# A spectral and attention stack on one core: the memory check split among output tiles, short projection runs joined, and the spectrum's PSUM ring undone

## The chip, the cores and the metric

The kernel runs on one core of a Trainium2 chip. The metric is device time in microseconds (us) of one execution. Five engines work side by side, each through its own instructions in order: PE (TensorE: matmuls; its weight loads are listed as PEld), DVE (VectorE), ACT (ScalarE), POOL (GpSimd) and SP (SyncE, which issues transfers here). They wait for each other by semaphores. Matmul results go to PSUM, a small memory of banks; the kernel takes buffers in it from pools with tags, and a tag with `bufs=2` is a ring of two buffers: the third tile waits until the first has been read. S1 to S6 below are regions of SBUF that stages share.

## The reference

Four layers with a residual each: A, B, A, B. Layer A is a Fourier filter over tokens and features. Layer B is attention in 64 segments of 32 tokens, in which 8 memory rows pass from each segment to the next.

```python
def _A_ref(x, w_r, w_i):
    X = rfft2(x.astype(float32))
    X = X * (w_r + 1j * w_i)
    return irfft2(X, s=(S, D)).astype(bfloat16)

def _B_ref(x, mem0, Wq, Wk, Wv, Wo, seg_len):
    mem = mem0
    for s in range(n_seg):
        h = concatenate([mem, x[segment s]])
        q, k, v = h @ Wq, h @ Wk, h @ Wv            # 32 heads of 128
        p = softmax(where(mask, q @ k.T * scale, -1e9))
        o = (p @ v) @ Wo
        mem = o[:, :M]                              # the next segment's memory
        outs.append(o[:, M:])
    return concatenate(outs)

x = A_x                                             # (1, 2048, 640)
x = x + A(layernorm(x)); x = x + B(layernorm(x))
x = x + A(layernorm(x)); x = x + B(layernorm(x))
```

The kernel doesn't run layer B segment by segment. It guesses every segment's memory, computes all segments at once, and then checks that the memory rows it got agree with the guess to 1 in 100; a flag sends the program into a slower general path where they don't. This is the memory check.

## The kernel before

Layer A, spectrum. For each of eight indices j: matmuls along the features (`along_d`), sums and differences on DVE (`combine`), matmuls across (`across`), multiplication with the weights on DVE (`filt`), `products` on DVE and POOL, and matmuls back (`back`). The accumulators of the first two and X take their buffers from one ring of three.

```python
def along_d(j, o):
    ab[j, o] = ps = pp.tile([128, 2, 512], FP32, name=f"ab{o}", tag="pg", bufs=3)
    ...                                       # 10 matmuls of 321 columns; for o == 1 a copy to SBUF by ACT
def combine(j):                               # L320, L321 on DVE
    ...
def across(j, sg):
    X[j, sg] = x = pp.tile([128, 2, 512], FP32, name="X", tag="pg", bufs=3)
    ...                                       # 4 matmuls of 321 columns
def filt(j, sg):                              # L337: two multiplications of X with the weights on DVE
    ...
def products(j):
    ...
    nc.vector.tensor_tensor(out=a[:, 0, :, :], ..., op=ALU.subtract)                                # L343
    (nc.gpsimd if pos[j] < 6 else nc.vector).tensor_tensor(out=a[:, 1, :, :], ..., op=ALU.add)      # L344
    if j:
        nc.gpsimd.tensor_tensor(out=sd[j][:, 0:2, :], ...)                                          # L346
        nc.gpsimd.tensor_tensor(out=sd[j][:, 2:4, :], ...)                                          # L347

for i in range(8 + 3):                        # the order on PE, ACT and DVE is this one
    j, last, done = [self.SEQ[k] if 0 <= k < 8 else None for k in (i, i - 1, i - 3)]
    if j is not None: along_d(j, 1)
    if rest is not None: back(rest, (2,)) ...
    if last is not None: across(last, 0); filt(last, 0)
    if j is not None: along_d(j, 0); combine(j)
    if last is not None: across(last, 1); filt(last, 1); products(last) ...
    rest = done
    if done is not None: back(done, (0, 1))
```

Layer B, heads. Keys and queries of a head are projected in five runs of columns each, the last one short; dependent work of the two heads before (score parts, sums, value groups) is merged between them.

```python
kruns = [(0, 502), (512, 1007), (1024, 1519), (1536, 2035), (2048, 2176)]

def chain(w, hh, ps, src, lo, hi):            # five matmuls, L918
    ...
def k_run(w, h, g_):                          # chain into a PSUM tile (ring of 3), DVE copies it out (L977)
def q_run(w, h, g_):                          # chain into the same ring, ACT scales it out (L962 and smaller ones)
def score_part(h, P, part):                   # L994 into "pss" (ring of 2), ACT Exp (L997), DVE mask (L998)
def sums_wide(P, Rb, g_):                     # last head: L1043, then Ln and Exp on ACT (L1045, L1046)
def value_group(h, P, Rb, oT, g_):            # L1053 into "pso" (ring of 2), DVE scales it out (L1062 to L1066)

dense += [lambda g_=g_: k_run(w, h, g_) for g_ in range(NG)]         # NG = 5
...
    dense += [lambda g_=g_: q_run(w, h, g_) for g_ in range(NG)]
vt = [lambda t=t: v_tiles(w, h // 2, t) for t in range(0, NT, 2)]    # L984
dense += vt[5:] if h % 2 else vt[:5]
...
merge(dense, parts + [g1[0], post[0], g1[1], post[1], g1[2], post[2], g1[3], g1[4]])   # spread evenly
...
elif h == H:                                  # after the last head: output tiles begun as filling
    merge(begin(), parts)
    b1 = begin()
    wide[0](); wide[1]()
    merge(b1[0:3], wide[2:5]); merge(b1[3:], groups)
    post[0]()
else:
    merge(begin(), groups)
```

Layer B, end. The check runs first, then the 16 output tiles (two half tiles of 32 matmuls each, L1209, added to x on DVE, L1219). In the first layer B each tile is normed and its first matmuls for the next layer A follow (`stage1_tile`, L273).

```python
def _b_mem_check(...):
    for c in range(5):
        for h in range(H):                    # 32 matmuls of 71 columns, L692
            nc.tensor.matmul(ps[:, :NM], lhsT=Wo_sb[:, h, c * 128:(c + 1) * 128], rhs=oTm[:, h, 0:NM], ...)
        for lo, hi, guess in gq_of(c):        # the guess subtracted on DVE, L697
            nc.vector.tensor_tensor(out=dl[:, lo:hi], in0=ps[:, lo:hi], in1=guess, op=ALU.subtract)
        nc.scalar.activation(out=sq[:], in_=dl[:], func=ACTF.Square)               # L700
        nc.scalar.activation(out=n2[:], in_=ps[:, 0:NC], func=ACTF.Square)         # L701
        nc.tensor.matmul(pe2[:, 0:NC], lhsT=ones_c[:, 0:1], rhs=sq[:], ...)        # L702
        nc.tensor.matmul(pn2[:, 0:NC], lhsT=ones_c[:, 0:1], rhs=n2[:], ...)        # L703
    ...                                       # verdict on DVE; range of the sums, L716 to L720

for t in range(16):                           # _FastOut.run
    for k in (2 * t, 2 * t + 1):
        self.accumulate(ps, k, lhs, ...)      # L1209
        nc.vector.tensor_tensor(out=x[:, t, c0:c0 + 320], in0=ps[:, 0:320], in1=x[...], op=ALU.add)
    if nxt is None: nc.sync.dma_start(out=self.xd[:, t, :], in_=x[:, t, :]); continue
    if t: nxt.stage1_tile(pa, "pss", xns[(t - 1) % 3], t - 1)
    ...                                       # statistics and norm of tile t
if nxt is not None: nxt.stage1_tile(pa, "pss", xns[15 % 3], 15)
```

Of the kernel before, what the change touches and what calls it, by code (L numbers as in the profile page):

```python
# [148 lines left out]
class _Cut:  # L149

    def __init__(self, t):
        self.t, self.o = t, 0
# [39 lines left out]
class LayerA:  # L192
# [83 lines left out]
    def spectrum(self, late_loads=()):  # L276
# [19 lines left out]
        self.pp = pp = tc.alloc_tile_pool(name=f"{self.lname}_ps2", bufs=1, space=PSUM)  # L296
# [4 lines left out]
        def along_d(j, o):  # L301
            ab[j, o] = ps = pp.tile([128, 2, 512], FP32, name=f"ab{o}", tag="pg", bufs=3)
            for ch in range(5):
                for c in range(2):
                    nc.tensor.matmul(ps[:, 1 - c if o else c, 0:NF], lhsT=YT[:, ch, 2 * j + c, :, :].rearrange("p s k -> p (s k)"), rhs=Fd[:, ch, o, :],  # L305
                                     start=(ch == 0), stop=(ch == 4))
            if o == 1 and j:
                ab[j, o] = dbs
                nc.scalar.copy(out=dbs, in_=ps[:, :, 0:NF])
# [13 lines left out]
        def across(j, sg):  # L323
            X[j, sg] = x = pp.tile([128, 2, 512], FP32, name="X", tag="pg", bufs=3)
# [14 lines left out]
        def products(j):  # L339
# [3 lines left out]
            nc.vector.tensor_tensor(out=a[:, 0, :, :], in0=t1[:, :, 0, :], in1=t2[:, :, 0, :], op=ALU.subtract)  # L343
            (nc.gpsimd if pos[j] < 6 else nc.vector).tensor_tensor(out=a[:, 1, :, :], in0=t1[:, :, 1, :], in1=t2[:, :, 1, :], op=ALU.add)  # L344
# [4 lines left out]
        def back(j, chunks):  # L349
            for ch in chunks:  # L350
                f0, f1 = CH[ch]
                m = f1 - f0
                if j == 0 and ch == 1:
                    psu = pp.tile([128, 2, 512], FP32, name="psu0", tag="pg", bufs=3)[:, 0, :].rearrange("p (e c k) -> p e c k", e=2, c=2)
                else:
                    psu = pp.tile([128, 2, 2, 128], FP32, name="psu2", tag="pu", bufs=2)
# [9 lines left out]
                for e in range(2):  # L366
                    (nc.vector.tensor_copy if j == 0 and ch == 1 else nc.scalar.copy)(out=UT[0:m, ch, e, :, j * 16:j * 16 + 16].rearrange("p s (c k) -> p s c k", c=2),
                                                                                in_=psu[0:m, e, :, :].rearrange("p c (s k) -> p s c k", k=8))

        with tc.manual_schedule(engines={nc.tensor.engine, nc.scalar.engine, nc.vector.engine}):  # L370
            rest = None
            for i in range(8 + 3):
                j, last, done = [self.SEQ[k] if 0 <= k < 8 else None for k in (i, i - 1, i - 3)]
                if j is not None:
                    along_d(j, 1)
                if rest is not None:
                    back(rest, (2,))
                    for _ in range(2):
                        if late:
                            late.pop(0)(UT[0:1, 0, 0, 0, rest * 16:rest * 16 + 1])  # L380
# [6 lines left out]
                if last is not None:  # L387
                    across(last, 1)
                    filt(last, 1)
# [3 lines left out]
                rest = done  # L393
                if done is not None:
                    back(done, (0, 1))
            back(rest, (2,))
            for f in late:
                f(UT[0:1, 0, 0, 0, 112:113])

    def tokens(self, x_dst, xn_dst, handoff=None):  # L400
# [8 lines left out]
        pp = self.pp  # L409
# [266 lines left out]
def _b_mem_check(tc, g, pj, pc, wk, oTm, mnb, gq_of, NM, NC, flag_col, sums=None):  # L676
    nc = tc.nc
    Wo_sb, ones_c = g["Wo_sb"], g["ones_c"]
    pe2, pn2 = pc[0][0:1, :], pc[1][0:1, :]
    cut = {}  # L680

    def tmp(name, p, n, dt=FP32):
        if not isinstance(wk, _Cut):
            return wk.tile([p, n], dt, name=name, tag=name, bufs=1)[:]
        if name not in cut:
            cut[name] = wk.f32(n) if dt == FP32 else wk.bf(n)
        return cut[name][0:p, :]

    for c in range(5):
        ps = pj.tile([128, 512], FP32, name="psm", tag="pj")  # L690
        for h in range(H):
            nc.tensor.matmul(ps[:, :NM], lhsT=Wo_sb[:, h, c * 128:(c + 1) * 128], rhs=oTm[:, h, 0:NM], start=(h == 0), stop=(h == H - 1))  # L692
        if mnb is not None:
            nc.scalar.copy(out=mnb[:, c, :], in_=ps[:, :NM])
        dl = tmp("dl", 128, NC)
        for lo, hi, guess in gq_of(c):
            nc.vector.tensor_tensor(out=dl[:, lo:hi], in0=ps[:, lo:hi], in1=guess, op=ALU.subtract)  # L697
        sq = tmp("sq", 128, NC, BF16)
        n2 = tmp("n2", 128, NC, BF16)
        nc.scalar.activation(out=sq[:], in_=dl[:], func=ACTF.Square)  # L700
        nc.scalar.activation(out=n2[:], in_=ps[:, 0:NC], func=ACTF.Square)  # L701
        nc.tensor.matmul(pe2[:, 0:NC], lhsT=ones_c[:, 0:1], rhs=sq[:], start=(c == 0), stop=(c == 4))  # L702
        nc.tensor.matmul(pn2[:, 0:NC], lhsT=ones_c[:, 0:1], rhs=n2[:], start=(c == 0), stop=(c == 4))  # L703
    e2 = tmp("e2", 1, NC)
    nc.vector.tensor_copy(out=e2[:], in_=pe2[:, 0:NC])
    viol = tmp("viol", 1, NC)
    nc.vector.scalar_tensor_tensor(out=viol[:], in0=pn2[:, 0:NC], scalar=-(CONV_TOL ** 2), in1=e2[:], op0=ALU.mult, op1=ALU.add)
    vmax = tmp("vmax", 1, 1)
    nc.vector.tensor_reduce(out=vmax[:], in_=viol[:], axis=AX.X, op=ALU.max)
    if sums is None:  # L710
        nc.vector.tensor_single_scalar(out=flag_col, in_=vmax[:], scalar=0.0, op=ALU.is_gt)
        return
    accR, accS = sums
    okw = tmp("okw", 128, accR.shape[1])
    ok2 = tmp("ok2", 128, 2, BF16)
    nc.vector.tensor_single_scalar(out=okw[:], in_=accR, scalar=INV_MAX, op=ALU.is_le)  # L716
    nc.vector.tensor_reduce(out=ok2[:, 0:1], in_=okw[:], axis=AX.X, op=ALU.min)
    nc.vector.tensor_single_scalar(out=okw[:], in_=accS, scalar=SUM_MAX, op=ALU.is_le)
    nc.vector.tensor_reduce(out=ok2[:, 1:2], in_=okw[:], axis=AX.X, op=ALU.min)
    nc.tensor.matmul(pe2[:, 0:2], lhsT=ones_c[:, 0:1], rhs=ok2[:], start=True, stop=True)  # L720
    ok = tmp("okq", 1, 2)
    nc.vector.tensor_single_scalar(out=ok[:], in_=pe2[:, 0:2], scalar=127.5, op=ALU.is_ge)
    okm = tmp("okm", 1, 1)
    nc.vector.tensor_reduce(out=okm[:], in_=ok[:], axis=AX.X, op=ALU.min)
    nc.vector.tensor_single_scalar(out=vmax[:], in_=vmax[:], scalar=0.0, op=ALU.is_le)
    nc.vector.tensor_tensor(out=vmax[:], in0=vmax[:], in1=okm[:], op=ALU.mult)
    nc.vector.tensor_single_scalar(out=flag_col, in_=vmax[:], scalar=0.5, op=ALU.is_lt)
# [38 lines left out]
def _b_full_pass(tc, g, lay, env, flag_col):  # L766
# [86 lines left out]
    with octx:  # L853
# [3 lines left out]
        _b_mem_check(tc, g, pj, (pcs[:, 0, :], pcs[:, 1, :]), wk, oTm, mnb, lambda c: [(0, lay.NC, gq[:, c, MR:NSEG * MR])], lay.NM, lay.NC, flag_col)  # L857
# [10 lines left out]
def _b_fast_pass(tc, g, bs, env, flag_col, nxt=None):  # L868
# [32 lines left out]
    if True:  # L901
# [198 lines left out]
        with tc.manual_schedule(engines={nc.tensor.engine, nc.scalar.engine, nc.vector.engine}):  # L1100
            for h in range(H + 2):
# [11 lines left out]
                if h < H:  # L1113
                    dense += [lambda g_=g_: k_run(w, h, g_) for g_ in range(NG)]
                    if h < 2:
                        dense.append(lambda: q_m(w, h))
                    else:
                        dense += [lambda g_=g_: q_run(w, h, g_) for g_ in range(NG)]
# [391 lines left out]
```

## Time and profile before

| | |
|---|---|
| time, median of 3 | 1636.85 us (1634.64 to 1639.93) |
| span of the profiled execution | 1635.0 us |
| PE busy | 1555.4 us, 95% |
| ACT, DVE, POOL busy | 51%, 49%, 17% |
| first spectrum, then tokens | about 35 to 92, 92 to 135 us |
| first layer B: heads, output tiles | about 135 to 687, 687 to 833 us |
| second spectrum, tokens | about 834 to 891, 891 to 938 us |
| second layer B: heads, output tiles | about 938 to 1490, 1490 to 1635 us |

A line of the timeline gives start, length, engine, line of the kernel, operation, what is written and read, its size and the count, and in brackets how long the engine stood idle before it and what ended that. Lengths of single matmuls overlap, so starts are compared. In the list of waits each line says who waited for whom, total us, times and the longest. "Issue" is idle time for which the profile shows no releaser.

### The profile page before, as it was taken

What the parts mean: (1) busy time and instruction counts of PE and PEld (TensorE: products, weight loads), DVE (VectorE), ACT (ScalarE), POOL (GpSimd) and SP (SyncE); (2) the same over time, 40 slices, a digit from 0 to 9 for tenths busy, and PEclk for the clock granted to TensorE, in tenths of its full rate; (3) what the DMA queues carried; (4) which work ended last, traced back from release to release, by engine and by line L of the source; (5) the groups of instructions that cost most, each with busy time, mean ns of one, the idle gap of its engine ahead of it and who ended that gap; (6) DMA issues with size and microseconds to landing.
All of it is one profiled execution on the core that took longest, in us unless ns stands there. A gap on an engine that the chain in (4) does not pass through costs nothing. (4 is left out here: it accounts for less than half of the span.)

```text
span 1635.0 us, 36218 instructions
## 1 busy us (share of the span) xinstructions
PE 1555.4 (95%) x14240; PEld 1072.1 (66%) x14241; DVE 800.1 (49%) x2254; ACT 836.4 (51%) x2522; POOL 275.7 (17%) x262
## 2 busy tenths in 40 slices
PE   4898999999999999899987899999999999999998
PEld 2566666666666667677755666666666667666775
DVE  5973454555545554533358625555545554544110
ACT  5374666666666666511124746666666666663000
POOL 0520121212121212100024101212121212111000
PEclk9999999999999999999999999999999999999999
DMA  4472334334434343824202713434434343446241
GB/s 157 145 278 87 100 134 144 135 135 139 151 117 154 117 161 121 268 93 118 77 15 95 257 31 126 135 135 140 151 117 153 118 160 122 140 144 214 69 132 52
DMA packets 167873, 218.05 MB, mean 133 GB/s; under 512 B 7374, under 2 KB 141836, under 8 KB 159756
## 3 DMA queue, kind: packets, MB, share of 16 engines
q1 hardware_dynamic: 167084, 213.34, 39.1%
q8 instruction: 113, 1.85, 0.5%
q0 software_dynamic: 608, 2.30, 0.4%
q14 instruction: 68, 0.56, 0.1%
HBM read 170.52 MB, written 45.09 MB: 132 GB/s over the span
## 5 line engine op out<-in xcount | busy, mean ns | idle before, releaser
L918 PEld LDWEIGHTS <-bB_S 128*128 128x128 bf16 x3180 | 261.1, 97 | 184.4 <-issue 4.3
L1062 DVE TENSOR_TENSOR bB_S<-pso,bB_S 128x480 bf16<-128x480 f32 (+1 forms) x320 | 189.4, 592 | 265.9 <-PE pso L1053 251.6
L997 ACT ACTIVATE bB_S<-pss 128x269 bf16<-128x269 f32 (+5 forms) x576 | 213.6, 385 | 192.6 <-PE pss L994 180.4
L1209 PE MATMUL psx<-Wo_sb,bB_S 128*128 128x320 bf16 x2048 | 288.2, 299 | 3.0 <-DMA bB_S<-oTx_d 3.0
L977 DVE CAST bB_S<-psk 128x495 bf16<-128x495 f32 (+3 forms) x320 | 191.4, 599 | 123.0 <-PE psk L918 92.3
L1209 PEld LDWEIGHTS <-bB_S 128*128 128x128 bf16 x2048 | 197.2, 98 | 79.6 <-DMA bB_S<-oTx_d 3.7
L998 DVE TENSOR_TENSOR bB_S<-bB_S,maskf 128x269 bf16<-128x269 bf16 (+5 forms) x576 | 163.0, 287 | 153.1 <-ACT bB_S L997 149.3
L1022 POOL TENSOR_TENSOR bB_S<-bB_S,bB_S 128x634 f32<-128x634 f32 x64 | 98.0, 1531 | 786.5 <-ACT bB_S L1018 786.5
L986 ACT CAST bB_S<-psv 128x512 bf16<-128x512 f32 (+1 forms) x288 | 160.5, 557 | 84.4 <-PE psv L984 84.1
L962 ACT ACTIVATE bB_S<-psq 128x480 bf16<-128x480 f32 x300 | 152.5, 508 | 98.8 <-PE psq L918 98.8
L918 PE MATMUL psk<-B2hT_S,bB_S 128*128 128x495 bf16 (+3 forms) x800 | 165.4, 343 | 2.3 <-DVE bB_S L977 2.1
L918 PE MATMUL psk<-B1hT_S,bB_S 128*128 128x495 bf16 (+3 forms) x800 | 165.3, 343 | 0.6 <-DVE bB_S L977 0.4
L984 PE MATMUL psv<-bB_S,B1hT_S 128*128 128x256 bf16 x1360 | 163.4, 273 | 0.2 <-DVE bB_S L977 0.2
L984 PE MATMUL psv<-bB_S,B2hT_S 128*128 128x256 bf16 x1360 | 163.4, 273 | 0.2 <-DVE bB_S L977 0.2
L994 PEld LDWEIGHTS <-bB_S 128*128 128x128 bf16 x1216 | 102.8, 97 | 90.5 <-issue 6.2
L918 PE MATMUL psq<-B2hT_S,bB_S 128*128 128x495 bf16 (+5 forms) x780 | 158.1, 336 | 0.1
L918 PE MATMUL psq<-B1hT_S,bB_S 128*128 128x495 bf16 (+5 forms) x780 | 158.0, 336 | 0.1
L994 PE MATMUL pss<-bB_S 128*128 128x132 bf16 (+8 forms) x1216 | 147.8, 215 | 2.8
L984 PEld LDWEIGHTS <-B2hT_S 128*128 128x128 bf16 x1360 | 128.8, 98 | 13.6 <-issue 0.3
L984 PEld LDWEIGHTS <-B1hT_S 128*128 128x128 bf16 x1360 | 128.8, 98 | 13.5 <-issue 0.3
L1053 PE MATMUL pso<-bB_S,bB_S 128*128 128x132 bf16 (+8 forms) x1216 | 119.6, 216 | 0.0
L1053 PEld LDWEIGHTS <-bB_S 128*128 128x128 bf16 x1216 | 91.2, 98 | 15.9 <-DVE oTmf L1063 0.5
(245 smaller groups left out, 1544.7 us busy)
## 6 DMA issues: line engine op xcount, KB each, us to landing
bB_S<-Rd SPq DMA_DIRECT2D x62, 1059.5 KB
oTx_d<-bB_S SPq DMA_DIRECT2D x60, 512.0 KB
bB_S<-oTx_d SPq DMA_DIRECT2D x56, 512.0 KB
bB_S<-in_B_Wq_dram SPq DMA_DIRECT2D x32, 320.0 KB
bB_S<-in_B_Wk_dram SPq DMA_DIRECT2D x32, 320.0 KB
bB_S<-in_B_Wv_dram SPq DMA_DIRECT2D x32, 320.0 KB
bB_S<-oTx_d SPq DMA_DIRECT2D x14, 384.0 KB
Wo_sb<-in_B_Wo_dram SPq DMA_DIRECT2D x4, 1280.0 KB
```

The costliest lines, as they stand in the source:

```text
L918: nc.tensor.matmul(ps, lhsT=w[:, ch, hh * 128:(hh + 1) * 128], rhs=src[:, ch, lo:hi], start=(ch == 0), stop=(ch == 4))
L962: nc.scalar.mul(out=qv[:, :, 0:SEG], in_=x_view(ps, o, n)[:, :, 1:SW], mul=scale)
L977: nc.vector.tensor_copy(out=KTs[h % 2][:, lo:hi], in_=ps[:, 0:hi - lo])
L984: nc.tensor.matmul(ps[:, i * 256:(i + 1) * 256], lhsT=hT[:, ch, st.hcol((t + i) * 128):st.hcol((t + i) * 128) + 128], rhs=w["Wv"][:, ch, : ...
L986: nc.scalar.copy(out=V[:, t:t + n, :].rearrange("p a b -> p (a b)"), in_=ps[:, 0:n * 256])
L994: nc.tensor.matmul(ps[:, off - o0:off - o0 + hi - lo], lhsT=KT[:, t * 128:(t + 1) * 128], rhs=QT[:, lo:hi], start=True, stop=True)
L997: nc.scalar.activation(out=E[:, 0:n], in_=ps[:, 0:n], func=ACTF.Exp)
L998: nc.vector.tensor_tensor(out=P[:, o0:o0 + n], in0=E[:, 0:n], in1=bs.mask[:, o0:o0 + n], op=ALU.mult)
L1022: nc.gpsimd.tensor_tensor(out=accS, in0=accS, in1=sums_sb, op=ALU.add)
L1053: nc.tensor.matmul(pso[:, lo - q0:hi - q0], lhsT=V[:, t, (h % 2) * 128:(h % 2 + 1) * 128], rhs=P[:, off:off + hi - lo], start=(i == 0), st ...
L1062: nc.vector.tensor_tensor(out=oT.rearrange("p (r s j) -> p r s j", r=16, j=2)[:, :, s0:s0 + ns, :], in0=byclass(po), in1=rx, op=ALU.mult)
L1209: self.tc.nc.tensor.matmul(ps[:, 0:320], lhsT=lhs(h, k // 2), rhs=self.g["Wo_sb"][:, h, c0:c0 + 320], start=(h == 0), stop=(h == H - 1))
```

## The change

Three things differ. (1) In layer B's heads the short key run is put into one item with the first long one, and so is the short query run; the order after the last head has more filling between the wide sums. (2) The memory check becomes a class with pieces: `prepare` and `begin` among the first output tiles, `block` and `vote` for each of the five parts. The guess is subtracted by a matmul with minus the identity into the same accumulator, the square is taken from PSUM, and the tolerance is applied to the guess, whose squares are made early. In the last layer all five parts stand among output tiles; in the first, two do, and three come after the last tile, ahead of its `stage1_tile`. The output loop now has a fixed order. (3) The spectrum of layer A has separate accumulators (ab0, ab1 and X, one buffer each) in place of the ring of three, does `back` in one go, and gives L343 to POOL for the first six indices; tokens use a pool of their own.

```diff
-            ab[j, o] = ps = pp.tile([128, 2, 512], FP32, name=f"ab{o}", tag="pg", bufs=3)
+            ab[j, o] = ps = pp.tile([128, 2, 512], FP32, name=f"ab{o}", tag=f"ab{o}")
...
-            X[j, sg] = x = pp.tile([128, 2, 512], FP32, name="X", tag="pg", bufs=3)
+            X[j, sg] = x = pp.tile([128, 2, 512], FP32, name="X", tag="X")
...
-            nc.vector.tensor_tensor(out=a[:, 0, :, :], in0=t1[:, :, 0, :], in1=t2[:, :, 0, :], op=ALU.subtract)
-            (nc.gpsimd if pos[j] < 6 else nc.vector).tensor_tensor(out=a[:, 1, :, :], in0=t1[:, :, 1, :], in1=t2[:, :, 1, :], op=ALU.add)
+            (nc.gpsimd if pos[j] < 6 else nc.vector).tensor_tensor(out=a[:, 0, :, :], in0=t1[:, :, 0, :], in1=t2[:, :, 0, :], op=ALU.subtract)
+            (nc.gpsimd if j else nc.vector).tensor_tensor(out=a[:, 1, :, :], in0=t1[:, :, 1, :], in1=t2[:, :, 1, :], op=ALU.add)
...
-                if rest is not None:
-                    back(rest, (2,))
...
                 if last is not None:
                     across(last, 1)
+                if i >= 3:
+                    done = self.SEQ[i - 3]
+                    back(done)
...
+                if last is not None:
                     filt(last, 1)
                     products(last)
...
+    def begin(self, acc=None):
+        if acc is not None:
+            nc.tensor.matmul(self.pe[:, self.NC:self.NC + 2], lhsT=self.g["ones_c"][:, 0:1], rhs=self.ok2[:], start=True, stop=True)
+        for c in range(5):
+            nc.tensor.matmul(self.pe[:, 0:self.NC], lhsT=self.g["minus_c"][:, 0:1], rhs=self.n2[:, c, :], start=(c == 0), stop=False)
+
+    def block(self, c):
...
         for h in range(H):
+            nc.tensor.matmul(ps[:, :NM], lhsT=self.g["Wo_sb"][:, h, c * 128:(c + 1) * 128], rhs=self.oTm[:, h, 0:NM], ...)
...
+        for i, (lo, hi, guess) in enumerate(guesses[:n]):
+            nc.tensor.matmul(ps[:, lo:hi], lhsT=self.minus[:], rhs=guess, start=False, stop=(i == n - 1), ...)
+        nc.scalar.activation(out=sq[:], in_=dl[:, 0:NC], func=ACTF.Square)
+
+    def vote(self, c):
+        self.tc.nc.tensor.matmul(self.pe[:, 0:self.NC], lhsT=self.g["ones_c"][:, 0:1], rhs=self.squares[c][:], start=False, stop=(c == 4))
...
-                    dense += [lambda g_=g_: k_run(w, h, g_) for g_ in range(NG)]
+                    def both(run):
+                        return [lambda: (run(w, h, NG - 1), run(w, h, 0))] + [lambda g_=g_: run(w, h, g_) for g_ in range(1, NG - 1)]
+                    dense += both(k_run)
+                    dense += [lambda: q_m(w, h)] if h < 2 else both(q_run)
...
-                    b1 = begin()
-                    wide[0]()
-                    wide[1]()
-                    merge(b1[0:3], wide[2:5])
-                    merge(b1[3:], groups)
+                    fill = begin()
+                    for i, f in enumerate(wide):
+                        f()
+                        for _ in range(2):
+                            (fill or groups).pop(0)()
...
+        early = {t: c for c, t in enumerate((3, 5) if nxt is not None else (3, 5, 7, 9, 11))}
...
+            if t == 2:
+                check.prepare(acc)
+            if t == 4:
+                check.begin(acc)
+            if t in early:
+                check.block(early[t])
+            if t - 1 in early:
+                check.vote(early[t - 1])
...
         if nxt is not None:
+            for c in range(len(early), 5):
+                check.block(c)
             nxt.stage1_tile(pa, "pss", xns[15 % 3], 15)
+            for c in range(len(early), 5):
+                check.vote(c)
+            check.result(flag_col, True)
```

## The prediction

> **What bounds the kernel now.** I read the page first, then busy time by stage, then the timeline inside the stages that the change edits, then the list of waits.
>
> ```profile
> PE 1555.4 (95%) x14240; PEld 1072.1 (66%) x14241; DVE 800.1 (49%) x2254; ACT 836.4 (51%) x2522; POOL 275.7 (17%) x262
> ```
>
> TensorE is busy 95% of the span and no other engine passes 51%. Where the missing 5% lie is told by the stages (columns: stretch, its length, then busy time of PE, PEld, DVE, ACT, POOL, the granted clock, DMA share, GB/s):
>
> ```profile
> 145.00:640.00 495.00, 492.71 (x4552) 331.98 (x4549) 244.95 (x731) 308.31 (x977) 88.71 (x58) 1.00 0.38 130
> ...
> 834.00:891.00 57.00, 47.29 (x316) 32.17 (x316) 48.28 (x57) 18.56 (x54) 29.16 (x24) 0.92 0.14 43
> ...
> 938.00:1460.00 522.00, 517.63 (x4793) 348.06 (x4793) 253.63 (x756) 321.56 (x1018) 91.77 (x60) 1.00 0.37 128
> ```
>
> The attention heads (the two long stretches, two thirds of the time) are TensorE alone: a matmul of 502 columns starts every 0.21 us. The spectrum (834 to 891) is a hand-over between PE and DVE: each is busy about 48 of 57 us. So in the heads only PE stalls and PE work count, and in the spectrum it is the length of the cycle PE, DVE, POOL.
>
> In the heads the timeline of PE shows one stall, in every second head:
>
> ```profile
> 1031.31 0.45 PE L918 MATMUL psk<-B2hT_S,bB_S 128*128 128x128 bf16 x5
> 1031.59 0.65 PE L994 MATMUL pss<-bB_S 128*128 128x141 bf16 x4
> 1032.08 1.22 PE L918 MATMUL psq<-B2hT_S,bB_S 128*128 128x502 bf16 x5
> ```
>
> The four score matmuls take 0.49 us to the next start; four such without a stall, at 670.92, take 0.23. They are two score parts in a row, only 0.28 us (the short key run) after the part before them; scores have two PSUM buffers, and the second part needs the one that ACT's Exp is still reading. The list of waits counts these:
>
> ```profile
> PEld L994 <- issue: 6.2, 30, 0.2
> ```
>
> Thirty, that is 15 heads in each layer. At the end of layer B the memory check stands alone on PE (layer 1 shown):
>
> ```profile
> 687.36 1.17 PE L692 MATMUL psm<-oTmf,Wo_sb 128*128 128x71 bf16 x31
> 689.60 0.19 PE L692 MATMUL psm<-oTmf,Wo_sb 128*128 128x71 bf16 x1 [1.07 <-DVE oTmf L1066]
> ...
> 694.65 1.21 PE L692 MATMUL psm<-oTmf,Wo_sb 128*128 128x71 bf16 x32
> ...
> 700.46 0.16 PE L720 MATMUL pc<-bB_S,ones_c 128*1 128x2 bf16 x1
> 700.56 3.30 PE L1209 MATMUL psx<-Wo_sb,bB_S 128*128 128x320 bf16 x23
> ...
> 829.31 0.44 PE L273 MATMUL ps<-bB_S 128*128 128x128 bf16 x5
> 832.64 0.72 PE L273 MATMUL ps<-bB_S 128*128 128x128 bf16 x5 [2.89 <-DVE bB_S L127]
> ```
>
> From 687.36 to 700.46 PE holds the check and 20 output matmuls, with waits on DVE and ACT in every block; 32 check matmuls alone take 1.2 us. At the other end PE idles 2.9 us for the norm of the last tile, and the next layer's first 20 matmuls then run at 0.28 us each instead of 0.14 (they span 833.98 to 839.5). The spectrum's cycle:
>
> ```profile
> 856.95 2.20 DVE L343 TENSOR_TENSOR A2gt_S<-A2tmp_S 128x642 f32<-128x642 f32 x1
> 859.08 1.54 DVE L337 TENSOR_TENSOR A2tmp_S<-X,A2tab_S 128x642 f32<-128x642 f32 x2
> ...
> 856.93 1.54 POOL L344 TENSOR_TENSOR A2gt_S<-A2tmp_S 128x642 f32<-128x642 f32 x1 [0.37 <-DVE A2tmp_S L337]
> ```
>
> DVE's L343 takes 0.83 when it runs first and 2.20 when POOL's L344 (1.54) started just before it; then the next product of X, and through the ring PE, come late. The step was 5.26 us (848.57 to 853.83) and becomes 6.71 (860.55 to 867.26).
>
> [...] 0.28 for 0.14 us after 2.9 us of idleness, and no fall inside the check, where PE has gaps of about 1 us at most. [...]
>
> **The change, part by part.**
>
> *Heads.* Key run 4 goes ahead of run 0 as one item, and so does query run 4. The list has 12 or 13 items for 17 dependent ones in place of 14 or 15, so more pairs of dependents stand together, but each pair now follows at least a long run (1.05 us) after the previous part, and Exp takes 0.4. The 30 stalls go: 30 x (0.49 - 0.23) = 7.8 us. No matmul is added or removed.
>
> *Check, layer 1.* I walk PE on the clock of the old trace. Up to 673.1 nothing differs. Each wide sum is now followed by two output items (1.09 us) in place of one, so PE doesn't wait for Ln and Exp (1.2 us a sum): about 1.1 us. The wait of PE for head 30's reciprocals (DVE at 679.39) stays. L716 and L717 (1.3 us) no longer stand between the last evictions, so those end at about 688.1, not 689.4. Then 41 output matmuls (1+4+4+32) at 0.136 end the fourth half tile at 693.8; in the old trace it ends at 703.7. Gain 9.9. Given back: two blocks of 32 matmuls at 33 ns plus two subtractions, 1.12 each, and seven votes at 0.12: 3.1. Three blocks (3.4) go where PE idled from 829.6 to 832.6, and the last stage-1 matmuls, votes and DVE's read of the vote bank delay the spectrum by about 0.6. But PE no longer idles, so I expect the full clock: 20 matmuls x 0.14 = 2.7 gained. Sum: 9.9 - 3.1 - 0.6 + 2.7 = 8.9 us.
>
> *Check, layer 2.* The same 9.9, less five blocks (5.6), votes and openings (1.2), all in the body: 3.1 us.
>
> *Spectrum, twice.* X gets one buffer of its own: PE can fill it only when DVE has left it, so DVE idles 0.85 us a step (0.06 + 4 x 0.138 + 0.2), as long as the L343 that goes to POOL. [...] POOL has 1.5 + 1.5 + 1.3 + 1.3 = 5.6 us a step, PE has 1.38 + 0.37 (wait) + 0.55 + 1.77 (the three chunks of "back" in one go, with 0.3 for a buffer) + 1.38 + 0.55 = 6.0. So 6.0 in place of 6.7 on four steps: 2.9 us. At the end "back" of index 7 waits for POOL, about as now. The walk gives 2.9 us a spectrum; as it hangs on POOL times that I have not seen together, I count 2.0: 4.0 us for both.
>
> Sum: 7.8 + 8.9 + 3.1 + 4.0 = 23.8; 1636.85 - 23.8 = 1613.
>
> **Rivals.**
>
> *The spectrum gets longer.* If POOL's L343 and L344 take 2.2 rather than 1.54 (the longest in the trace), POOL needs 7.0 a step and lags; "back" and the products of the last indices wait. For it: POOL has four operations a step and the chain crosses three engines with one X. Against it: POOL's 1.54 is steady where DVE isn't in its way. It would cost about 3 us each where I count 2 gained: 1623.
>
> *The stall in the heads moves.* The short query run's three small ACT evictions now come ahead of the long run's, just before two score parts in a row; if Exp is late there, the same 0.26 returns. For it: ACT has about 2 us of work in that stretch. Against it: by the durations in the old trace the buffer is free 0.1 to 0.2 us in time. It would make 1621.
>
> *A hidden transfer shows.* The output stage starts 10 us earlier, but its tables are issued only after the last head's values (DFT table at 688.6), and the DMA engines are full until 705. The first stage-1 matmuls would come at 693.8. For it: that issue time doesn't move. Against it: that table is the first in the queue. It could take 0 to 5 us from layer 1: up to 1618.
>
> **Range and chances.** All three rivals together come to about 1636, unlikely at once; one of the first two is 1621 to 1623. If instead the spectrum gives the full 2.9 (1.8 more in all) and the clock stays up in further places (it also stands below full, at 0.84, from 880.7 to 891.5 and at 0.85 from 82.6 to 94.0), 1605 to 1608. Eight in ten: 1603 to 1625. Faster by 2% means below 1604.1: 0.12. Slower by 2%, above 1669.6, needs a new wait of 55 us: 0.02. Within 2%: 0.86.
>
> **What would show it.** Heads: "PEld <- issue" on the score line falls from 30 to about 0. Check: no stretch of PE with check matmuls alone; three blocks just before the last stage-1 matmuls; first 20 spectrum matmuls at 0.14. Spectrum: combine to combine 6.0 us, L343 on POOL at 1.54. The prediction is wrong if score matmuls still wait, if stage 1 of tile 0 waits for a DMA, or if POOL operations take 2 us.

## The result and the profile after

The changed kernel takes 1619.08 us (median of 4 runs, 1614.60 to 1620.72) beside 1636.61 us for the kernel before; the ratio is 0.9887 with a 95% interval of 0.9859 to 0.9914. That is 17.5 us gained where the prediction summed 23.8. The profiled execution of the changed kernel is the longest of its four, span 1619.0 us against 1635.0. Its busy times, from the page:

```profile
PE 1548.0 (96%) x14260; PEld 1068.8 (66%) x14261; DVE 777.2 (48%) x2219; ACT 836.0 (52%) x2530; POOL 295.7 (18%) x278
```

Matmuls are up by 20 and PE's busy time is down by 7.4 us (1555.4 before), the span by 16.1. So some 8.7 us of idle time went, and the rest is time that was counted as busy: a score matmul that stands for its buffer counts as busy while it stands (0.65 in place of 0.40 us for four, 30 times). The stretches between fixed points of PE's program, read from the starts of single matmuls in both traces, say where the time came from:

| stretch (us) | before | after | gain | predicted |
|---|---|---|---|---|
| heads of layer 1, first key matmul to first output matmul | 515.30 | 511.12 | 4.2 | 3.9 |
| heads of layer 2 | 517.25 | 512.79 | 4.5 | 3.9 |
| first to 129th output matmul, layer 1 | 35.72 | 29.90 | 5.8 | 9.9 |
| the same, layer 2 | 34.90 | 29.00 | 5.9 | 9.9 |
| 129th to last output matmul, layer 1 | 125.20 | 128.04 | -2.8 | -3.1 |
| the same, layer 2 | 121.57 | 128.38 | -6.8 | -6.8 |
| last output matmul of layer 1 to 21st transform of layer A | 10.13 | 7.66 | 2.5 | 2.1 |
| first spectrum, first transform to first inverse matmul | 57.10 | 57.93 | -0.8 | 2.0 |
| second spectrum, 21st transform to first inverse matmul | 52.18 | 51.71 | 0.5 | 2.0 |
| first inverse matmul to first key matmul, both layers | 122.91 | 119.56 | 3.4 | 0 |

Heads, check pieces and the end of layer 1 came as predicted. Two things did not: the start of the output stage gained 6 us a layer in place of 10, and the spectra gained nothing. A line that the prediction did not have, 3.4 us after the spectra, hides part of that; 2.8 of it lie in layer 2, where 20 query matmuls ran partly at half clock before (5.98 us, granted clock 0.72 from 938.1 to 944.1) and don't now (1.00 from 926.9 to 931.3), a difference of 1.6.

The score line in the groups of PE's weight loads (columns: count, busy us, mean ns, idle before, and what ended it) has no "issue" item left, where the waits before counted 6.2 us in 30 times:

```profile
L1013 PEld LDWEIGHTS <-bB_S 128*128 128x128 bf16 x1216 | 99.7, 97 | 84.4
```

PE's timeline (start, length, what, count, and in brackets the idle time before and its releaser), at the end of the heads, at the first product of layer A's first stage (L273), and at the end of layer 1:

```profile
677.51 0.45 PE L1233 MATMUL psx<-Wo_sb,bB_S 128*128 128x320 bf16 x2 [2.98 <-DMA bB_S<-oTx_d]
...
679.63 2.34 PE L1233 MATMUL psx<-Wo_sb,bB_S 128*128 128x320 bf16 x8
...
686.73 5.74 PE L1233 MATMUL psx<-Wo_sb,bB_S 128*128 128x320 bf16 x41 [0.27 <-DVE bB_S L1081]
693.80 0.44 PE L273 MATMUL ps<-bB_S 128*128 128x128 bf16 x5 [1.33 <-DVE lnst L104]
...
822.53 1.20 PE L711 MATMUL psm<-oTmf,Wo_sb 128*128 128x71 bf16 x32
...
825.86 0.45 PE L273 MATMUL ps<-bB_S 128*128 128x128 bf16 x5
826.24 0.26 PE L725 MATMUL pc<-bB_S,ones_c 128*1 128x70 bf16 x3
827.04 4.28 PE L305 MATMUL ab<-A2tab_S,A2YT_S 128*128 128x321 bf16 x30 [0.54 <-ACT A2YT_S L274]
```

Read it from the bottom: the blocks at 822.5 fill the wait on the last norm, and 30 transforms then take 4.28 us, 0.14 each, where the first 20 took 0.28 before (granted clock 1.00 from 827.0 to 831.5; before, 0.51 from 833.98 to 839.5). Further up, the check no longer stands alone between 686.7 and 693. But at 674.5 PE waits 2.98 us for a load; after it eight output matmuls take 2.34 us, 0.29 each: half clock (granted clock 0.50 from 679.6 to 682.0). In layer 2 the same wait is 3.17 us (0.50 from 1468.5 to 1472.5). Before, it was 1.50 in layer 1 and 1.55 in layer 2, with no half clock after it (1.00 from 680 to 690 and from 1483.4 to 1490):

```profile
680.02 0.31 PE L1209 MATMUL psx<-Wo_sb,bB_S 128*128 128x320 bf16 x1 [1.50 <-DMA bB_S<-oTx_d]
```

The two matmuls that wait are the ones of heads 28 and 29 for the first output tile, which the compiler's ordering draws ahead of the value groups, because the heads and the output stage are two separately ordered parts of the program.

In the spectrum, this is the timeline of several engines at the end of the second one (L318 is the last combine, L412 the first inverse matmul):

```profile
867.48 1.56 DVE L337 TENSOR_TENSOR A2tmp_S<-X,A2tab_S 128x642 f32<-128x642 f32 x2 [1.63 <-issue]
868.96 0.81 DVE L318 CAST A2tmp_S<-ab 128x642 bf16<-128x642 f32 x1
...
871.63 0.49 POOL L1283 MEMSET B2hT_S<- 128x85 bf16 x4
872.06 1.71 POOL L344 TENSOR_TENSOR A2gt_S<-A2tmp_S 128x642 f32<-128x642 f32 x1
872.29 1.54 DVE L337 TENSOR_TENSOR A2tmp_S<-X,A2tab_S 128x642 f32<-128x642 f32 x2
...
873.89 0.72 PE L332 MATMUL X<-A2tmp_S,A2tab_S 128*128 128x321 bf16 x4 [1.71 <-DVE A2tmp_S L337]
874.66 1.56 DVE L337 TENSOR_TENSOR A2tmp_S<-X,A2tmp_S 128x642 f32<-128x642 f32 x2 [0.82 <-PE X L332]
875.12 1.32 POOL L347 TENSOR_TENSOR A2tmp_S<-A2gt_S 128x642 bf16<-128x642 f32 x1
...
876.50 0.33 PEld L361 LDWEIGHTS <-A2tmp_S 128*128 128x128 bf16 x4 [0.28 <-POOL A2tmp_S L347]
...
881.48 0.71 PE L412 MATMUL psg<-A2gt_S,A2UT_S 128*128 128x321 bf16 x4 [0.91 <-DVE A2UT_S L363]
```

The steps did shrink (combine to combine 6.13 us, 6.72 before; the last combine came 2.2 us earlier after the first). But from the last combine to the inverse it is 12.5 us now. PE waits for the one X buffer (1.71), DVE then waits for PE (0.82), and `back` of index 6 (counted from 0; the prediction calls it index 7) starts when POOL's L347 ends at 876.44.

### The profile page after: what moved, and what is told of

It is laid out like the page before. It is cut to its first block, busy times and chain, and to the rows that moved or that the text cites. A ratio compares the mean times of both kernels' runs of the same rounds, so it can differ in the third digit from the quotient of the medians.

```text
span 1619.0 us, 36256 instructions
## 1 busy us (share of the span) xinstructions
PE 1548.0 (96%) x14260; PEld 1068.8 (66%) x14261; DVE 777.2 (48%) x2219; ACT 836.0 (52%) x2530; POOL 295.7 (18%) x278
## 5 line engine op out<-in xcount | busy, mean ns | idle before, releaser
L1016 ACT ACTIVATE bB_S<-pss 128x269 bf16<-128x269 f32 (+5 forms) x576 | 203.9, 386 | 202.3 <-PE pss L1013 189.7
L1017 DVE TENSOR_TENSOR bB_S<-bB_S,maskf 128x269 bf16<-128x269 bf16 (+5 forms) x576 | 159.1, 288 | 162.2 <-ACT bB_S L1016 162.2
L981 ACT ACTIVATE bB_S<-psq 128x96 bf16<-128x96 f32 x300 | 152.4, 508 | 91.3 <-PE psq L937 90.3
L937 PE MATMUL psq<-B2hT_S,bB_S 128*128 128x495 bf16 (+5 forms) x780 | 153.2, 336 | 0.0
L937 PE MATMUL psq<-B1hT_S,bB_S 128*128 128x495 bf16 (+5 forms) x780 | 153.2, 336 | 0.0
L1013 PE MATMUL pss<-bB_S 128*128 128x132 bf16 (+8 forms) x1216 | 133.2, 216 | 0.1
```

The costliest lines, as they stand in the source:

```text
L937: nc.tensor.matmul(ps, lhsT=w[:, ch, hh * 128:(hh + 1) * 128], rhs=src[:, ch, lo:hi], start=(ch == 0), stop=(ch == 4))
L981: nc.scalar.mul(out=qv[:, :, 0:SEG], in_=x_view(ps, o, n)[:, :, 1:SW], mul=scale)
L1013: nc.tensor.matmul(ps[:, off - o0:off - o0 + hi - lo], lhsT=KT[:, t * 128:(t + 1) * 128], rhs=QT[:, lo:hi], start=True, stop=True)
L1016: nc.scalar.activation(out=E[:, 0:n], in_=ps[:, 0:n], func=ACTF.Exp)
L1017: nc.vector.tensor_tensor(out=P[:, o0:o0 + n], in0=E[:, 0:n], in1=bs.mask[:, o0:o0 + n], op=ALU.mult)
```

## The experiments

Where the lines below give stretches, they are those of the table above.

**The parts alone.** Three kernels hold one part of the change each.

*Joined runs.* Edit, on the kernel before:

```diff
-dense += [lambda g_=g_: k_run(w, h, g_) for g_ in range(NG)]   # and q_run likewise
+dense += both(k_run)                                          # and both(q_run)
```

> The kernel before with the joined key and query runs alone; check, output stage and spectrum are the old ones. Theory (the stall of the score matmuls was worth its full time in the heads): the score line loses its 30 waits put down to 'issue', each attention stretch is 4 to 4.5 us shorter, time 8 to 9 us below the kernel before (about 1628, ratio 0.995). Rival (the stall moves to ACT's backlog, or the heads pass their gain to a wait at their end): 2 to 5 us, and if the heads' end is what loses, the first output matmuls after the heads wait 3 us for the load of oTx_d here already.

Measured: 1628.36 us, ratio 0.9958 (0.9942 to 0.9975), 6.9 us. The heads are 4.3 and 5.6 us shorter and the issue waits of the score line are gone. At their end the load of oTx_d holds PE for 2.04 and 2.42 us (1.50 and 1.55 before), and in layer 2 half clock follows it (four output matmuls take 1.27 us, 0.70 or 0.71 ahead of the wait). So the stall was worth its full time, and in this profile about 3 us of it are given back between the first and the 129th output matmul. That is no price of shorter heads, as the kernel with the key runs alone shows below.

*Check in pieces.* The class of pieces, the new order after the last head and the fixed output loop, on the kernel before:

```diff
-_b_mem_check(tc, g, pj, pc, s1, oTm, None, ..., sums=(accR, accS))
+check = _MemCheck(tc, g, pj, pc, s1, oTm, None, ...)
...
+        out.run(x, lhs_of, psx, first, HPRE, pa, xns, check, (accR, accS), flag_col)
```

> The kernel before with the check in pieces (and the new order after the last head) alone. Theory (in the changed kernel the new order after the last head runs into the load of heads 28 and 29 and then into the half clock, which gives back some 6 us of what the check brings): 4 to 7 us below the kernel before (about 1631), with a wait of PE of about 3 us on oTx_d at the end of the heads in both layers. Rival (the wait belongs to the shorter heads, not to the new order): 10 to 12 us below (about 1625), with the wait at 1.5 us as before.

Measured: 1626.04 us, ratio 0.9940 (0.9923 to 0.9956), 9.8 us. My theory of the moment was wrong: the waits on oTx_d are 1.58 and 1.89 us, hardly longer than before. Yet layer 1 comes to its 129th output matmul after 29.2 us, as late as the whole change, and layer 2 after 25.4. PE's timeline in layer 1 shows another load:

```profile
691.71 2.88 PE L1239 MATMUL psx<-Wo_sb,bB_S 128*128 128x320 bf16 x20
698.22 0.44 PE L273 MATMUL ps<-bB_S 128*128 128x128 bf16 x5 [3.64 <-DMA bB_S<-cT]
```

cT is the table of layer A's first stage; only layer 1 has it.

*Spectrum.* Edit, on the kernel before: one buffer each for ab0, ab1 and X, `back` in one go, L343 to POOL.

```diff
-x = pp.tile([128, 2, 512], FP32, name="X", tag="pg", bufs=3)
+x = pp.tile([128, 2, 512], FP32, name="X", tag="X")
-nc.vector.tensor_tensor(out=a[:, 0, :, :], ...)
+(nc.gpsimd if pos[j] < 6 else nc.vector).tensor_tensor(out=a[:, 0, :, :], ...)
```

> The kernel before with the changed spectrum alone. Theory (the shorter step is given back at the last three indices): within 2 us of the kernel before, each spectrum's step at 6.1 us in place of 6.7, and the stretch from the last combine to the first inverse matmul 2 to 3 us longer. Rival (the spectrum gives what the prediction counted, and the loss lies elsewhere): 4 us below, 1632.5.

Measured: 1635.37 us, ratio 0.9999 (0.9990 to 1.0008). The spectrum part gives nothing. First to last combine is 38.9 us in both spectra (41.1 before), last combine to inverse 12.5 and 13.7 (10.6 and 10.8 before). Some of these ends met half clock: before, the granted clock was 0.84 from 880.7 to 891.5, and eleven matmuls of `back` took 2.57 us. In the second spectrum of the kernel with the joined runs seven of them take 0.94 us, and the old spectrum's end takes 9.8 us; the new one's takes 12.5 (granted clock 1.00 from 868 to 882 in the change): the 2.2 us of the steps come back as 2.7. DVE's and PE's timelines of the old end at full clock (joined runs alone):

```profile
875.32 0.81 DVE L318 CAST A2tmp_S<-ab 128x642 bf16<-128x642 f32 x1
...
882.00 0.94 PE L365 MATMUL psu<-A2tab_S,A2tmp_S 128*128 128x256 bf16 x7 [0.99 <-POOL A2tmp_S L347]
...
885.12 1.02 PE L418 MATMUL psg<-A2gt_S,A2UT_S 128*128 128x321 bf16 x5
```

From the last combine to the point where POOL's L347 lets `back` of index 6 go on is 6.7 us here and 7.5 in the change (868.96 to 876.50): 0.9 of the 2.7. From there to the inverse is 3.1 us here and 5.0 in the change: 1.9.

The three parts together are 6.9 + 9.8 + 0.2 = 16.9 us by their ratios, the whole change 18.5 by its own (0.9887 of 1636.6); within the intervals the parts simply add.

*Joined key runs without the query runs:*

```diff
-dense += [lambda g_=g_: k_run(w, h, g_) for g_ in range(NG)]
+dense += [lambda: (k_run(w, h, NG - 1), k_run(w, h, 0))] + [lambda g_=g_: k_run(w, h, g_) for g_ in range(1, NG - 1)]
```

> The kernel before with the joined key runs alone, the query runs as they were. Theory (the stall is that of the second of two score parts 0.28 us apart, behind the short key run): the 30 waits of the score line go, each attention stretch is 4 to 5 us shorter, as with both joined. Rival (the parts that stand close are set by the whole list, and the short query run makes such pairs too): about half of the 30 waits are left.

Measured: the heads take 511.3 and 512.7 us, as with both joined, and the score line has no issue waits; 1626.11 us in one run. The short key run alone made the stall; joining the query runs does no more for the heads. The waits on oTx_d are 0.58 and 1.54 us here, and the first 129 output matmuls take 34.7 and 35.0 us, about as before (35.7 and 34.9), though the heads are as short as with both joined.

**The start of the output stage.** The next three kernels build on the change, each on the one before.

*One order for heads and output:*

```diff
-with tc.manual_schedule(engines={nc.tensor.engine, nc.scalar.engine, nc.vector.engine}):
-    for h in range(H + 2):
+octx.enter_context(tc.manual_schedule(engines={...}))    # stays open to the end of out.run
+for h in range(H + 2):
```

> The changed kernel, with the heads and the output stage in one fixed order instead of two, so that no output matmul of heads 28 and 29 is drawn ahead of the value groups of head 30. Theory (that matmul's wait for its load, 2.98 and 3.17 us, and the half clock that follows are the loss at the heads' end): the wait on oTx_d goes, the two stretches between the first and the 85th output matmul fall from 21.7 and 22.6 us to about 17, the time to about 1609. Rival (the value groups need DVE and the reciprocals anyway, so the wait only changes its name): 1616 to 1619, with new waits on DVE or ACT of about the same length.

Measured: 1619.08 us, ratio 0.9898 (0.9881 to 0.9914): no gain over the change. The wait on oTx_d is gone and two others stand in PE's timeline of layer 1:

```profile
677.03 0.41 PE L1072 MATMUL pso<-bB_S,bB_S 128*128 128x132 bf16 x4 [1.69 <-DVE oTmf L1082]
...
694.28 0.69 PE L273 MATMUL ps<-bB_S 128*128 128x128 bf16 x5 [4.02 <-DMA bB_S<-cT]
694.76 6.40 PE L1233 MATMUL psx<-Wo_sb,bB_S 128*128 128x320 bf16 x26
```

DVE in its turn waits for the reciprocals of head 30, which go through memory (its timeline):

```profile
676.24 0.66 DVE L1081 TENSOR_TENSOR bB_S<-pso,bB_S 128x480 bf16<-128x480 f32 x1 [5.65 <-DMA bB_S<-Rd]
```

So the wait on oTx_d was the first of three; PE was only held a little later. First to 85th output matmul falls to 18.9 and 21.0 us (17 expected). But in layer 1 first to 129th is 29.8 us, as in the change, and the 26 output matmuls after the wait on cT take 6.40 us, 0.25 each, nearer to the 0.28 of half clock than to the 0.14 of full clock. The rival was right, though the last wait is a load and not an engine. cT is issued at 685.7, because its place in SBUF is that of the value vectors, and lands 8.5 us later.

*First-stage products one tile later*, on the kernel with one order:

```diff
-if t:
-    nxt.stage1_tile(pa, "pss", xns[(t - 1) % 3], t - 1)
+if t > 1:
+    nxt.stage1_tile(pa, "pss", xns[(t - 2) % 3], t - 2)
```

> The kernel with one fixed order, and the first product of each normed tile (128-column matmuls with the table cT) put two output tiles behind its tile in place of one. Theory (once the wait on oTx_d was gone, PE ran into the table cT, which can only be loaded after the last value matmul: 4.02 us of wait and 5.5 us of half clock in one layer): both go, the stretch from the 85th output matmul of layer 1 to the last one shrinks from 141.6 to about 135, the time to about 1612.5. Rival (PE is ahead of something else too, DVE's norms or the block loads, and the wait changes its name once more): 1617 to 1619.

Measured: 1613.84 us, ratio 0.9881 (0.9847 to 0.9914). The time's interval overlaps that of the kernel with one order; the profile does not leave it open. The 85th to last output matmul of layer 1 takes 134.2 us (141.6), and PE's timeline has no break where cT was waited for:

```profile
682.84 15.42 PE L1233 MATMUL psx<-Wo_sb,bB_S 128*128 128x320 bf16 x111
```

First to 129th output matmul is now 25.3 us in both layers (29.8 and 27.2 with one order); the prediction had 35.7 - 9.9 = 25.8. Two things besides the load are in that: in layer 1 one first-stage product (0.3 us) now stands behind the stretch, and the last output matmul to the 21st transform takes 8.6 us for 7.7; layer 2 has no such products, and of its 1.9 us about 1.5 are half clock by an estimate from the kernel with one order: 16 matmuls from 1472.05 on take 3.36 us there, the same 16 of layer 1, from 678.60 on, 1.87. So the walk was about right for PE, and what it lacked were the loads.

*Value groups of head 31 before those of head 30*, on the kernel with the later products:

```diff
-oT[h - 2] = oTs[h % 2]
+vh = h - 2 if h < H else 2 * H - 1 - h     # then vh for h - 2 in groups and store
+oT[vh] = oTs[vh % 2]
```

> As late_stage1, and the value groups of head 31 (whose reciprocals come from PE's wide sums) before those of head 30 (whose reciprocals come through a store and a load). Theory (the 1.69 us wait on DVE at the end of the heads is the round trip of head 30's reciprocals): that wait and the half clock after it in layer 2 go, the stretch from the first to the 85th output matmul is 17 us in both layers (18.9 and 21.0 with one order), time about 5 us below late_stage1 (1607). Rival (DVE's own work on ten groups bounds that stretch): at most 1 us below late_stage1, with short waits on DVE in nearly every group.

Measured: 1610.03 us, ratio 0.9858 (0.9830 to 0.9887), 3.8 us less. First to 85th output matmul is 18.1 us in both layers (19.1 in the kernel before it), first to 129th 24.1 (25.3), so the profiles show 2.4 us of the 3.8, between the two expectations; the spectra, which this edit does not touch, differ by 3.6 between the two profiles. The long wait is gone, but DVE's work on the groups shows:

```profile
672.97 0.41 PE L1072 MATMUL pso<-bB_S,bB_S 128*128 128x132 bf16 x4 [0.87 <-DVE oTmf L1082]
673.93 0.41 PE L1072 MATMUL pso<-bB_S,bB_S 128*128 128x132 bf16 x4 [0.56 <-DVE oTmf L1082]
```

The half clock in layer 2 is absent too, but it already was in the kernel before, where that wait is 1.82 us, and it is back in the kernel below that joins these edits with those of the spectrum (first to 85th 19.8 us there; eight output matmuls take 1.93 us at 1459.56 and four more 1.27, where eight take 1.25 in its layer 1). It is not shown to be this edit's doing.

**The end of layer 1.** All five blocks among the output tiles, none for the last norm, on the changed kernel:

```diff
-early = {t: c for c, t in enumerate((3, 5) if nxt is not None else (3, 5, 7, 9, 11))}
+early = {t: c for c, t in enumerate((3, 5, 7, 9, 11))}
```

> The changed kernel with all five blocks of the check among the output tiles of layer 1 too, so that none is left for the wait on the last norm. Theory (a block is worth its time twice over there: it fills the wait, and it keeps the clock up for the transforms that follow): from the last output matmul to the 20th transform 10 us in place of 7.7, from the 128th to the last output matmul 3.4 us more, time 5.5 to 6 us above the changed kernel (about 1624). Rival (the clock falls or not whatever stands there): 3 us above it.

Measured: 1624.81 us, ratio 0.9943 (0.9923 to 0.9963) where the change has 0.9887 (0.9859 to 0.9914). Among the tiles the blocks cost 4.0 us more, and last output matmul to 21st transform is 9.9 us in place of 7.7, together 6.2 (5.7 by the times, about 9 by the ratios). PE's timeline:

```profile
827.30 0.71 PE L273 MATMUL ps<-bB_S 128*128 128x128 bf16 x5 [3.15 <-DVE bB_S L127]
828.64 6.37 PE L305 MATMUL ab<-A2tab_S,A2YT_S 128*128 128x321 bf16 x30 [0.63 <-ACT A2YT_S L274]
```

The wait of 3.15 us is back and 30 transforms take 6.37 us for 4.28. A block in that wait saved its own time, and with the blocks there the transforms ran at full clock (granted clock 1.00 from 827.0 to 831.5 in the change).

**The spectrum's end.** Three small edits on the changed kernel:

```diff
-X[j, sg] = x = pp.tile([128, 2, 512], FP32, name="X", tag="X")
+X[j, sg] = x = pp.tile([128, 2, 512], FP32, name="X", tag="ab1" if pos[j] == 7 and sg else "X")
+if j == 0 and ch == 1:
+    psu = pp.tile([128, 2, 512], FP32, name="psu0", tag="ab0")[:, 0, :].rearrange(...)
...   (the zeroing of the gaps of hT goes from begin back to memory)
```

> The changed kernel, with three edits at the end of the spectrum: the last X gets a bank that the transforms no longer need, so does one chunk of the last 'back', and the zeroing of the gaps of hT stands after the spectrum again. Theory (the shorter step is lost at the end to X's single buffer, to POOL's late start on index 6 behind that zeroing, and to the two buffers of 'back'): from the last combine to the first inverse matmul 1 to 1.5 us shorter in each spectrum, without the half clock in the first up to 3 us; time 2 to 4 us below the changed kernel (1615 to 1617). Rival (POOL's four products of the last two indices bound the end whatever PE finds): under 0.5 us each, no difference in time.

Measured: 1615.85 us, ratio 0.9886 (0.9857 to 0.9916), no difference from the change; its first spectrum's end takes 13.0 us where the change's takes 13.7, with a granted clock of 0.50 from 84.8 to 88.0 in the change's. Together with the edits of the three kernels above:

> swap and tail together. Theory: the gains add, since they lie in different stages: about 1604 us, ratio to the kernel before 0.980. Rival (the rivals of swap and tail both hold): 1611 to 1613.

Measured: 1608.83 us, ratio 0.9845 (0.9817 to 0.9873), 1.2 us below the kernel without the three edits and not to be told from it. Its second spectrum needs 11.7 us from the last combine to the inverse in place of 12.5. So the buffers and the zeroing were 0.8 us of the 2.7, all of it behind POOL's L347, which still ends 7.5 us after the last combine. Of the other 1.9, then, 0.9 are POOL's lateness. In the change it works almost without a pause from 865.93 on, and ahead of the two sums of index 6 it now has L344 of that index as well (1.71 us; the diff's `if j`). The remaining 1.1 lie in the last `back`, where the inverse now waits for DVE's copies (0.91); which edit makes them was not tested.

*The old ring with L343 on POOL*, on the kernel with the swapped value groups:

```diff
 # the spectrum of before: tag "pg" with three buffers, back in (0, 1) and (2,)
-nc.vector.tensor_tensor(out=a[:, 0, :, :], in0=t1[:, :, 0, :], in1=t2[:, :, 0, :], op=ALU.subtract)
+(nc.gpsimd if pos[j] < 6 else nc.vector).tensor_tensor(out=a[:, 0, :, :], in0=t1[:, :, 0, :], in1=t2[:, :, 0, :], op=ALU.subtract)
```

> The kernel of run 'swap', with the spectrum of before (one ring of three buffers for transforms and X, 'back' in two parts) in which only L343 goes to GpSimd. Theory (the single X buffer keeps DVE idle 0.85 us a step, and the DVE chain at the end is what the shorter step runs into; the move of L343 to GpSimd alone is the useful part of the spectrum change): the step falls from 6.7 to 5.7 us, GpSimd's four operations, the end stays within a microsecond of its 9.8 to 10.8, first to last combine 37.5 in place of 38.9, each spectrum 2 to 4 us shorter than in 'swap', time about 1605. Rival (GpSimd falls behind, 'back' waits for it, and the end grows by what the steps lose, as with the single X): first combine to first inverse matmul within 0.7 us of the 51.4 of 'swap', no difference in time.

Measured: 1604.96 us, ratio 0.9822 (0.9801 to 0.9842), the fastest here, 1.8% below the kernel before. First to last combine is 34.6 us (38.9): the first steps behind the opening one take 4.4 us, the last 5.7. There POOL sets the pace, with four operations one behind the other; DVE waits for it (timeline of several engines, second spectrum):

```profile
851.30 1.55 POOL L343 TENSOR_TENSOR A2gt_S<-A2tmp_S 128x642 f32<-128x642 f32 x1
...
852.81 1.54 POOL L344 TENSOR_TENSOR A2gt_S<-A2tmp_S 128x642 f32<-128x642 f32 x1
...
854.43 1.32 POOL L346 TENSOR_TENSOR A2tmp_S<-A2gt_S 128x642 bf16<-128x642 f32 x1
...
854.79 1.56 DVE L337 TENSOR_TENSOR A2tmp_S<-X,A2tab_S 128x642 f32<-128x642 f32 x2 [1.23 <-POOL A2gt_S L344]
855.71 1.32 POOL L347 TENSOR_TENSOR A2tmp_S<-A2gt_S 128x642 bf16<-128x642 f32 x1
...
856.99 1.57 POOL L343 TENSOR_TENSOR A2gt_S<-A2tmp_S 128x642 f32<-128x642 f32 x1
```

The end is longer still, 13.7 and 14.3 us (in part at half clock: in the second spectrum 12 matmuls of `back` take 2.78 us from 863.85 on, and seven 0.94 from 866.82 on), but the sum from first combine to inverse is 48.3 in the second spectrum where the kernel with the swapped value groups has 51.4, and the old spectrum, with the joined runs, 50.9. So the move of L343 was worth having (2.6 us here), and what the change did beside it threw its worth away: the single buffers, `back` in one go and L344 of index 6 on POOL, which these runs do not take apart.

## Why the prediction held, and where it did not

The time fell inside the range, and the size of the gain was 17.5 us for 23.8. By its own steps:

- *Heads, 7.8 us:* right. 8.6 measured between the same two matmuls (4.18 + 4.46), the 30 waits gone. The kernel with the key runs alone shows that this came from the short key run, as the prediction said.
- *Pieces given back, 3.1 and 6.8 us:* right, 2.8 and 6.8.
- *End of layer 1, 2.7 - 0.6:* right, 2.5. The prediction expected full clock because PE would not idle; the kernel without blocks there loses both terms (a wait of 3.15 us, and 6.37 us for 30 transforms in place of 4.28).
- *"the fourth half tile at 693.8", gain 9.9 a layer:* this step failed. It measured 5.8 and 5.9. As work of PE, at 0.136 us an output matmul (eight start from 684.84 to 685.93 before), it was about right (10.4 and 9.7 of gain with the first-stage products one tile later, 0.3 of the 10.4 being the product that moved), but the walk let PE go on wherever PE was free. Three transfers end in this stretch: the load of heads 28 and 29, the reciprocals of head 30, and cT. The walk kept the wait for the reciprocals ("stays"), left out the load of oTx_d, though the old timeline has it with 1.50 us, and took cT for hidden, as it was behind the old check. The third rival named cT, "0 to 5 us", and its argument against, that the table is first in its queue, missed the point (the DMA share was 0.91 to 1.16 in every 2 us from 688 to 704 before, as that rival has it): it is issued only 1 to 2 us after the last value matmul. It is worth 3.1 to 4.0 us of wait where PE gets there early (3.14 in the kernel with the spectrum's small edits, whose wait on oTx_d was 2.17), and half clock with it (after it 26 output matmuls in 6.40 us with one order and 21 in 4.69 with the check alone, 0.25 and 0.22 each); in the change the wait on oTx_d and its half clock stand before it and take its place.
- *Spectrum, 2 x 2.0 us:* this step failed. The step length was right (6.0 predicted, 6.13 measured; DVE idles 1.63 us of it, not the 0.85 of the prediction, whose terms add up to 0.81), POOL's operations were as steady as hoped (1.55 and 1.32 us, one a spectrum 1.71), and so the first rival, with POOL at 2.2, did not occur. What failed is the sentence "At the end 'back' of index 7 waits for POOL, about as now". It waits for POOL 0.9 us longer, counted from the last combine, and the work behind that wait takes 1.9 us more, which the walk left out. The end grew from 9.8 to 12.5 us at full clock, more than the steps gained.
- *Not in the sum:* 3.4 us behind the spectra. Of these 1.6 are the 20 matmuls that met half clock in one profile and not in the other. Another 0.6, in layer 1, come with the change's spectrum (59.5 us there in every kernel with it, 60.0 to 60.3 in the four with the old one); 1.2 stay open. None of it was predicted: it is luck for the total, and without it the miss would be 10 to 11 us.
- *The second rival,* a stall that moves within the heads, did not occur.

What stays open: why the load of heads 28 and 29 lands later in some executions than in others. The wait on it was 2.98 and 3.17 us in the change's profile, 2.20 and 2.46 in the kernel with all blocks among the tiles, and 2.17 and 1.70 in the one with the spectrum's small edits, and all three have the same heads. In the spectrum it stays open what each of the other edits beside L343 costs.

## What to carry to other kernels

When work is moved away from in front of the next stage, list every transfer that this stage needs, and from each its earliest issue; the removed work may have hidden several, and taking away the first wait only shows the next. A pipeline is worth its length from the first to the last product: a shorter step on one engine counts only if the engines that drain it get there sooner too. And the 3 us wait of PE at the end of layer 1 was worth filling twice here, once for itself and once for the clock after it: 30 transforms took 6.37 us behind the open wait and 4.28 behind the filled one.

## What was not expected of the hardware

The length of a wait did not tell whether half clock would follow. After 1.70 us on a load (the kernel with the spectrum's small edits, layer 2) eight output matmuls took 2.34 us; after 1.89 us (the check in pieces alone, layer 2) eight took 1.25. In the old check, with waits of up to 1.07 us between 687 and 700, the granted clock stayed at 1.00. The wait of 1.71 us at the end of the spectrum stands in both spectra of the change. In the second, the four matmuls behind it take 0.72 us (shown above, at 873.89) and the granted clock is 1.00 from there to 877.00; in the first they take 1.26, and it is 0.50 from 84.81 to 88.00:

```profile
84.81 1.26 PE L332 MATMUL X<-A1tmp_S,A1tab_S 128*128 128x321 bf16 x4 [1.71 <-DVE A1tmp_S L337]
```

What decides between the two was not shown. The mean granted clock differed between executions too: of the change's four runs the slowest (1620.72) had 0.995 and the fastest (1614.60) 0.999.

DVE's long L343 is back at the end of the fastest kernel, where that of index 6 is still DVE's while POOL works off its backlog. It starts 0.16 us after POOL's L344 and takes 2.09 us; in the kernel before, at 846.35, it started 0.10 us ahead of L344 and took 0.83:

```profile
858.50 1.56 POOL L344 TENSOR_TENSOR A2gt_S<-A2tmp_S 128x642 f32<-128x642 f32 x1
858.66 2.09 DVE L343 TENSOR_TENSOR A2gt_S<-A2tmp_S 128x642 f32<-128x642 f32 x1
```

L337 took 0.81 to 0.83 us in all its 64 executions of the kernel before, those beside POOL's operations among them.
